# A hand-given instruction order extended through the weight fold and its seam, with TensorE in program order behind it

## The chip, the cores and the metric

One core of one Trainium2 chip. The metric is the device time of one execution in microseconds (us). Every kernel was run several times beside runs of the kernel before on the same chip. Quoted times are medians of the runs; times inside an execution count from the start of its span. A run more than 1.5% above the fastest of its kernel is called slow and is left out of ratios. A ratio is the mean time of one kernel's fast runs over that of the other kernel's fast runs of the same rounds, so it is not quite the ratio of the medians quoted.

In lines of the profile PE is TensorE, PEld its weight loads, DVE VectorE, ACT ScalarE, POOL GpSimd and SP the queue of transfers; L810 is line 810 of that kernel's source. A line of a timeline reads: start and length in us, engine, line, operation, result<-operands, shapes, count; in brackets the engine's idle time just before, and what ended it.

## The reference

```python
def phi(x):                      # polysketch features: products of two sketches, r = 8
    a = einsum('rd,bhsd->bhsr', S1, x); b = einsum('rd,bhsd->bhsr', S2, x)
    return einsum('bhsi,bhsj->bhsij', a, b).reshape(..., r * r)
q_p, k_p = phi(q), phi(k)        # q, k, v: 4 batches, 4 heads, 1088 rows, 32 columns
kv, z = einsum('bhsf,bhsd->bhfd', k_p, v), sum(k_p, axis=2)
x = num(q_p, kv) / (den(q_p, z) + 1e-6)      # then heads side by side: x is 4352 x 128
out = (((x @ w1) * (x @ w2)) @ w3) @ w_out   # d_ff 1024, d_model 128
```

The kernel computes `w3 @ w_out` once (the fold, result `w3o`), so that the end is `((x@w1)*(x@w2)) @ w3o`. It works in groups of 512 rows of x: two halves of each of four batches, then one last group of 256 rows. "x of (1,0)" is the attention output of batch 1, half 0. It is what the third group's products wait for. The way there: on the k side come two small products T and N, which VectorE splits into parts (Ta, Tb; Na, Nb), and kz, the sum over k's features and v; on the q side phi makes the features ph, which TensorE transposes and multiplies by kz to x. A group has 8 "a,b pairs" (`ffn_ab`: two products, a copy on ScalarE, a multiplication on VectorE) and 8 "o products" (`ffn_o`, with `w3o`).

## The kernel before

The w3 weights arrive as raw words. ScalarE makes two tiles of them (`words`), VectorE joins them (`join`, `add`), TensorE transposes (`w3_t`), ScalarE copies, TensorE multiplies by w_out (`w3_mm`):

```python
def words():                                   # in convert(): ScalarE, two passes
    nc.scalar.mul(x["c"], hi.bitcast(F32), 2.0 ** -112)
    nc.scalar.mul(x["m"].bitcast(I32), lo.bitcast(U32), 2.0 ** -29)
...
def w3_t(i):
    ps = psum.tile([128, CW // 128, 128], F32, tag="h", bufs=3, name="ps_wt")
    for c in range(CW // 128):
        nc.tensor.transpose(ps[:, c], w3c[i][:, c * 128:(c + 1) * 128], ident)
    nc.scalar.copy(w3T[ko][:, c0:c0 + CW // 128], ps)
def w3_mm(ko):
    for c in range(NC):
        nc.tensor.matmul(ps, w3T[ko][:, c], wo[:, c], start=(c == 0), stop=(c == NC - 1))
    nc.scalar.copy(w3o[:, ko], ps)
```

A hand-written list of steps (`run_all`) gives the order of the first part. Behind it the source merges streams of steps, and a scheduler may reorder. Dependencies of order, without any semaphore, chain each engine's instructions of the first part, and those behind may only not pass them.

```python
traced = nc.cur_bb.bb.instructions
first_part = len(traced)
run(merge(ffn_steps(1, 16), k_steps(1), w_out))        # the fold; 16 o products are held back
run(merge(ffn_steps(None, 4), q_main(1, 0)))           # the seam: o products beside x of (1,0)
run(merge(ffn_steps(2, 6), q_main(1, 1), rest_steps(1) + k_steps(2)))   # the third group
... # five more groups, last output
for n, ins in enumerate(traced):
    if ins.engine in ordered:
        if ins.engine in last:
            tc.add_manual_dep(ins, last[ins.engine].name, behind, reason="order")
        if n < first_part:
            last[ins.engine] = ins
```

## Time and profile before

| | before |
|---|---|
| time, median of the runs beside the change | 302.19 us |
| span of the profiled run; mean granted TensorE clock | 299.0 us; 0.994 |
| first w3 transpose; last pass of the last `w3_mm` | 59.3; 106.5 us |
| last pass of x of (1,0); of (1,1) | 118.1; 151.5 us |

A line of a table of stretches reads: stretch, its length, then the busy time of TensorE, its weight loads, VectorE, ScalarE and GpSimd, each with its number of instructions, then the granted TensorE clock, the share of DMA and its GB/s.

### The profile page before, as it was taken

The numbers are of one execution on the slowest core, as the hardware profiler recorded it, in microseconds if no ns is written. First come the engines' busy times: TensorE is split into PE (matmuls) and PEld (weight loads), VectorE is DVE, ScalarE is ACT, GpSimd is POOL, SyncE is SP. The second block draws the span as 40 slices with busy tenths as digits, with TensorE's granted clock in tenths as the row PEclk, the third lists the DMA queues.
The fourth block names the chain that finished last, engine by engine and source line by source line (L and its number), as shares of the span: only waits on it lengthen the run. The fifth ranks groups of instructions, "written<-read, shape, count | busy, mean of one in ns | idle before, by whom it ended". The sixth has DMA issues, their size and how long they took to land.

```text
span 299.0 us, 5582 instructions
## 1 busy us (share of the span) xinstructions
PE 282.7 (95%) x2214; PEld 159.8 (53%) x2214; DVE 207.6 (69%) x523; ACT 117.1 (39%) x226; POOL 7.5 (3%) x12
## 2 busy tenths in 40 slices
PE   7987799589999999999999999999999999999994
PEld 5876343267767774545644435464444444444572
DVE  6989779999998985699579329864862583453131
ACT  4634665667886322320242322122423323223122
POOL 0000000000000010010010001000100000000000
PEclk9999999979999999999999999999999999999999
DMA  5649996456744002200100200020002002002020
GB/s 164 211 99 311 254 309 252 134 160 201 246 123 134 0 2 35 71 2 10 30 0 0 35 2 1 2 37 0 2 0 35 2 0 35 1 2 35 0 35 18
DMA packets 28729, 22.37 MB, mean 75 GB/s; under 512 B 20000, under 2 KB 25248, under 8 KB 28704
## 3 DMA queue, kind: packets, MB, share of 16 engines
q1 hardware_dynamic: 28704, 22.03, 26.8%
q8 instruction: 17, 0.28, 0.4%
q14 instruction: 8, 0.07, 0.1%
HBM read 19.80 MB, written 2.23 MB: 74 GB/s over the span
## 4 chain that ended last, share of the span: by engine, by line
PE 80%; DVE 11%; ACT 3%; DMA 2%; issue 1%; SPq 1%; DVEq 0%
PE ps_o L875 19%; PE a_ps L862 19%; PE b_ps L866 18%; PE ps_kvz L557 5%; PE ps_w3o L428 5%; PE ps_x L818 3%; PE ps_wt L421 2%; PE ps_c L725 2%; PE ps_ph L807 2%; DMA k_sb<-in_k_dram 1%; DMA raw<-in_moe_w_dram 1%; PE ps_ab L504 1%; DVE g_k L301 1%; DVE w3c L285 1%; PE ps_c L738 1%
## 5 line engine op out<-in xcount | busy, mean ns | idle before, releaser
L868 DVE TENSOR_TENSOR ab<-ffa,b_ps 128x512 f32<-128x512 f32 (+1 forms) x72 | 47.1, 655 | 64.7 <-PE b_ps L866 62.9
L864 ACT COPY ffa<-a_ps 128x512 f32<-128x512 f32 (+1 forms) x72 | 40.4, 562 | 98.1 <-PE a_ps L862 98.0
L862 PE MATMUL a_ps<-xT,w 128*128 128x512 f32 (+1 forms) x144 | 71.9, 581 | 1.0 <-ACT xT L822 0.7
L866 PE MATMUL b_ps<-xT,w 128*128 128x512 f32 (+1 forms) x144 | 70.3, 570 | 0.0
L875 PE MATMUL ps_o<-ab,w3o 128*128 128x512 f32 (+1 forms) x144 | 70.0, 582 | 0.1
L866 PEld LDWEIGHTS b_ps<-xT,w 128*128 128x128 f32 x144 | 27.2, 190 | 30.1 <-issue 24.9
L875 PEld LDWEIGHTS ps_o<-ab,w3o 128*128 128x128 f32 x144 | 25.3, 189 | 23.9 <-issue 21.6
L862 PEld LDWEIGHTS a_ps<-xT,w 128*128 128x128 f32 x144 | 24.9, 190 | 23.5 <-issue 14.3
L809 ACT COPY pT<-ps_ph 128x512 f32<-128x512 f32 (+1 forms) x18 | 9.2, 565 | 21.0 <-PE ps_ph L807 21.0
L428 PEld LDWEIGHTS ps_w3o<-wo,w3T 128*128 128x128 f32 x128 | 16.5, 205 | 1.5 <-issue 1.2
L428 PE MATMUL ps_w3o<-wo,w3T 128*128 128x128 f32 x128 | 17.0, 289 | 0.0
L269 ACT ACTIVATE cv_c<-raw 128x512 f32<-128x512 f32 x22 | 14.9, 679 | 2.9 <-DVE w3c L282 1.5
L270 ACT ACTIVATE cv_m<-raw 128x512 int32<-128x512 uint32 x22 | 15.0, 681 | 1.8 <-DVE w3c L285 1.5
L421 PE MATMUL ps_wt<-ident,w3c 128*128 128x128 f32 x64 | 10.2, 288 | 4.7 <-DVE w3c L285 4.7
L215 PE MATMUL idle_ps<-zeros 128*128 128x256 bf16 x88 | 12.7, 309 | 1.7 <-DVE zeros L210 1.7
L822 ACT COPY xT<-ps_x 128x512 f32<-128x512 f32 (+1 forms) x9 | 5.1, 563 | 19.0 <-PE ps_x L818 19.0
L421 PEld LDWEIGHTS ps_wt<-ident,w3c 128*128 128x128 f32 x64 | 7.5, 147 | 8.7 <-ACT cv_c L269 4.2
L215 PEld LDWEIGHTS <-zeros 128*128 128x128 bf16 x88 | 9.6, 112 | 3.8 <-DVE zeros L210 1.7
L701 POOL TENSOR_TENSOR q<-qT,q 128x512 f32<-128x512 f32 x5 | 5.9, 1183 | 208.6 <-ACT q L697 208.6
L423 ACT COPY w3T<-ps_wt 128x512 f32<-128x512 f32 x16 | 9.2, 585 | 4.9 <-PE ps_wt L421 4.6
L807 PEld LDWEIGHTS ps_ph<-ident,ph 128*128 128x128 f32 x68 | 7.9, 142 | 5.8 <-issue 4.0
L285 DVE CUSTOM_DVE_ANT_0 w3c<-w3c,cv_m 128x1024 uint16<-128x1024 uint16 x16 | 10.8, 682 | 0.0
(182 smaller groups left out, 343.9 us busy)
## 6 DMA issues: line engine op xcount, KB each, us to landing
raw<-in_moe_w_dram SPq DMA_DIRECT2D x20, 512.0 KB, 5.0
qh<-in_q_dram SPq DMA_DIRECT2D x4, 544.0 KB, 5.8
k_sb<-in_k_dram SPq DMA_DIRECT2D x4, 512.0 KB, 5.2
out_dram<-oT SPq DMA_DIRECT2D x32, 64.0 KB, 1.9
kh<-in_k_dram SPq DMA_DIRECT2D x12, 128.0 KB, 6.4
v_sb<-in_v_dram SPq DMA_DIRECT2D x12, 128.0 KB, 5.1
raw<-in_moe_w_out_dram SPq DMA_DIRECT2D x2, 512.0 KB, 7.7
v_sb<-in_v_dram SPq DMA_DIRECT2D x1, 512.0 KB, 4.9
```

Source lines behind the costliest of these rows:

```text
L215: nc.tensor.matmul(idle_ps[:, :n], zeros[:, :128], zeros[:, :n], start=True, stop=True)
L269: nc.scalar.mul(x["c"], hi.bitcast(F32), 2.0 ** -112)
L270: nc.scalar.mul(x["m"].bitcast(I32), lo.bitcast(U32), 2.0 ** -29)
L421: nc.tensor.transpose(ps[:, c], w3c[i][:, c * 128:(c + 1) * 128], ident)
L428: nc.tensor.matmul(ps, w3T[ko][:, c], wo[:, c], start=(c == 0), stop=(c == NC - 1))
L557: nc.tensor.matmul(out[h * D:(h + 1) * D], lhs, rhs, start=start, stop=stop, skip_group_check=True)
L807: nc.tensor.transpose(ps[:, j * 128:(j + 1) * 128], s["ph"][:, j, 2 * p:2 * p + 2].rearrange("p h i j -> p (h i j)"), ident)
L862: nc.tensor.matmul(a_ps[:, :n], w1[:, cols], xT[key], start=True, stop=True)
L864: nc.scalar.copy(a_sb[:, :n], a_ps[:, :n])
L866: nc.tensor.matmul(b_ps[:, :n], w2[:, cols], xT[key], start=True, stop=True)
L868: nc.vector.tensor_mul(ab[:, :n], a_sb[:, :n], b_ps[:, :n])
L875: nc.tensor.matmul(o_ps[g][:, :n], w3o[:, c], ab_sb.pop((g, c))[:, :n], start=c == 0, stop=c == NC - 1)
```

## The change

Its intent: close TensorE's two gaps at the start of the fold (3.2 and 1.2 us, with a drop of the clock), and order the rest so that no switch between kinds of products is wasted. The hand-written list now goes on through the fold and the seam up to x of (1,0). Behind it TensorE alone keeps program order, and each group's last products come together.

```diff
-        st = []
-        for k in range(len(tiles) + 2):
-            for part, lag in ((0, 0), (1, 1), (2, 2)):
...
+        rounds = []
+        for k in range(len(tiles) + 3):
+            st = [tiles[k][0]] if k < len(tiles) else []      # words
+            if 0 < k <= len(tiles):
+                st += tiles[k - 1][1:3]                        # join, add
+            if k > 2:
+                st += tiles[k - 3][3]                          # w3_t, w3_mm
+            rounds.append(st)
...
+    run_all([g[0], *R[3], g[1], *R[4], *R[5], g[2], *R[6], *R[7], o0[0], *R[8], g[3], *R[9], o0[1], ...
+             *R[17], o0[5], k_kp0, *R[18], o0[6], k_gs0, k_kp1, *R[19], k_kv0, k_gs1, *R[20], k_kv1, k_rg, k_rv, o0[7],
+             k_fin1, g[6], k_next, k_Tm, o1[0], k_Tp, q_tr, q_grid, o1[1], k_Nm, q_lead, g[7], k_Np, q_rem, k_kz, o1[2], ay1, ay2,
+             split, o1[3], o1[4], dens, o1[5], dens2, o1[6], o1[7], phi, phT, nd])
     first_part = len(traced)
-    run(merge(ffn_steps(1, 16), k_steps(1), w_out))
-    run(merge(ffn_steps(None, 4), q_main(1, 0)))
-    run(merge(ffn_steps(2, 6), q_main(1, 1), rest_steps(1) + k_steps(2)))
...
+    def group(g, left, *others):
+        st = ffn_steps(g, left)
+        n = max(len(st) - 4, 0)
+        run(merge(st[:n], *others))
+        run(st[n:])
+    group(2, 6, q_main(1, 1), rest_steps(1) + k_steps(2))
...
-            if n < first_part:
+            if n < first_part or ins.engine == nc.tensor.engine:
```

In the list `g[c]` is the c-th a,b pair of the second group, `o0` and `o1` are the o products of the first and second group, `R[k]` is a round of the fold, `k_` steps are those of batch 1's k, and the rest are those of x of (1,0).

More of the change, by code (lines that the diff above doesn't have):

```diff
@@ L442, in w_out_steps @@
                 continue
-            words, join, add = convert(n, dst, signs=False)
-            tiles.append(([(0.6, words)], [(0.4, join), (0.3, add)], after))
-        st = []
-        for k in range(len(tiles) + 2):
-            for part, lag in ((0, 0), (1, 1), (2, 2)):
-                if 0 <= k - lag < len(tiles):
-                    st += tiles[k - lag][part]
-        return st
+            tiles.append(convert(n, dst, signs=False) + [[f for _, f in after]])
+        rounds = []
[6 more added lines that the diff above has]
+            rounds.append(st)
+        return rounds
     kz_done = {}
@@ L932, in run @@
             f()
-    w_in, w_out = w_in_steps(), w_out_steps()
+    w_in, rounds = w_in_steps(), w_out_steps()
     fs = lambda steps: [f for _, f in steps]
@@ L943 @@
     pause = lambda n: lambda: idle(n)
-    out_st, w_out = fs(w_out[:7]), w_out[7:]
+    out_st = sum(rounds[:3], [])
     run_all([sk_words, sketch_pairs, nat0, nat1, peak, sketch_T, tr0, tr1, ab0, ab1, r_nat, r_tr, first, second,
@@ L950 @@
              out_st[0], n_dens2, f[4], out_st[1], n_phi, f[5], *out_st[2:4], f[6], n_phT, n_nd, *out_st[4:7], f[7]])
+    (k_peak, k_first, k_second, k_tr0, k_tr1, k_ab, k_kp0, k_gs0, k_kv0, k_kp1, k_gs1, k_kv1, k_rg, k_rv,
+     k_fin1, k_next, k_Tm, k_Tp, k_Nm, k_Np, k_kz) = fs(k_steps(1))
+    q_tr, q_grid, q_lead, q_rem, ay1, ay2, split, dens, dens2, phi, phT, nd = fs(q_main(1, 0))
+    g = fs(ffn_steps(1, 16))
+    o0, o1 = ([lambda g=g, c=c: ffn_o(g, c) for c in range(NC)] for g in range(2))
+    pend.clear()
+    R = rounds
+    run_all([g[0], *R[3], g[1], *R[4], *R[5], g[2], *R[6], *R[7], o0[0], *R[8], g[3], *R[9], o0[1], *R[10], *R[11], o0[2],
+             g[4], *R[12], k_peak, o0[3], *R[13], k_first, *R[14], k_second, g[5], *R[15], o0[4], k_tr0, *R[16], k_tr1, k_ab,
+             *R[17], o0[5], k_kp0, *R[18], o0[6], k_gs0, k_kp1, *R[19], k_kv0, k_gs1, *R[20], k_kv1, k_rg, k_rv, o0[7],
+             k_fin1, g[6], k_next, k_Tm, o1[0], k_Tp, q_tr, q_grid, o1[1], k_Nm, q_lead, g[7], k_Np, q_rem, k_kz, o1[2], ay1, ay2,
+             split, o1[3], o1[4], dens, o1[5], dens2, o1[6], o1[7], phi, phT, nd])
     traced = nc.cur_bb.bb.instructions
     first_part = len(traced)
-    run(merge(ffn_steps(1, 16), k_steps(1), w_out))
-    run(merge(ffn_steps(None, 4), q_main(1, 0)))
-    run(merge(ffn_steps(2, 6), q_main(1, 1), rest_steps(1) + k_steps(2)))
-    run(merge(ffn_steps(3, 6), q_main(2, 0)))
-    run(merge(ffn_steps(4, 6), q_main(2, 1), k_steps(3)))
-    run(merge(ffn_steps(5, 6), q_main(3, 0)))
-    run(merge(ffn_steps(6, 6), q_main(3, 1)))
-    run(merge(ffn_steps(7, 6), q_rest()))
+    def group(g, left, *others):
[4 more added lines that the diff above has]
+    group(2, 6, q_main(1, 1), rest_steps(1) + k_steps(2))
+    group(3, 6, q_main(2, 0))
+    group(4, 6, q_main(2, 1), k_steps(3))
+    group(5, 6, q_main(3, 0))
+    group(6, 6, q_main(3, 1))
+    group(7, 6, q_rest())
     run(ffn_steps(8, 2))
```

## The prediction

> **What bounds the kernel now.** I read first the busy shares in 40 slices, to see which engine is full where; then a table of three stretches of my own choosing; then TensorE's and VectorE's instructions in order of time inside them. The page:
>
> ```profile
> PE   7987799589999999999999999999999999999994
> DVE  6989779999998985699579329864862583453131
> PEclk9999999979999999999999999999999999999999
> L868 DVE TENSOR_TENSOR ab<-ffa,b_ps 128x512 f32<-128x512 f32 (+1 forms) x72 | 47.1, 655 | 64.7 <-PE b_ps L866 62.9
> ```
>
> A slice is 7.5 us. TensorE is full from the ninth slice on, and VectorE nearly full from the seventh to the fourteenth (45 to 105 us), the fold of w3 and w_out. VectorE's idle time is nearly all waiting for TensorE, and lies later. The stretches: the fold, its seam to the third group's products, and the third group (columns: length, then busy time of each engine and its instructions).
>
> ```profile
> 54.20:106.60 52.40, 47.75 (x485) 35.43 (x484) 49.41 (x114) 35.36 (x64) 0.00 (x0) 0.97 0.48 142
> 106.60:119.70 13.10, 13.01 (x99) 7.11 (x97) 8.63 (x25) 3.54 (x7) 1.16 (x1) 1.00 0.12 21
> 119.70:153.00 33.30, 33.30 (x362) 17.03 (x361) 25.86 (x67) 8.45 (x16) 1.16 (x1) 1.00 0.11 26
> ```
>
> In the fold both engines are above 90%. In the third group TensorE never stops, and VectorE is at 78%. Why TensorE stops in the fold, from its timeline:
>
> ```profile
> 55.03 1.02 PE L866 MATMUL b_ps<-xT,w 128*128 128x512 f32 x2
> 59.26 0.63 PE L421 MATMUL ps_wt<-ident,w3c 128*128 128x128 f32 x4 [3.20 <-DVE w3c L285]
> 61.09 1.12 PE L421 MATMUL ps_wt<-ident,w3c 128*128 128x128 f32 x4 [1.20 <-DVE w3c L285]
> 62.00 3.09 PE L428 MATMUL ps_w3o<-wo,w3T 128*128 128x128 f32 x16
> ```
>
> It waits 3.2 and 1.2 us for converted w3 tiles, because VectorE did the next batch's k work between them. The 16 passes of L428 that follow take 2.9 us from start to start of the next kind and 1.8 us elsewhere: the clock had dropped (0.66 in the stretch 60 to 65 us). The third group's VectorE work, at its end:
>
> ```profile
> 138.20 1.22 DVE L798 TENSOR_TENSOR ph<-ay,bs 128x1024 f32<-128x1024 f32 x1
> 146.01 0.17 DVE L301 TENSOR_REDUCE g_pair<-ps_T 128x1 f32<-128x8 f32 x1 [1.48 <-PE ps_T L338]
> 149.26 0.17 DVE L301 TENSOR_REDUCE g_pair<-ps_N 128x1 f32<-128x8 f32 x1 [1.05 <-PE ps_N L338]
> 152.28 0.45 DVE L719 STREAM_TRANSPOSE ay_A<-ps_a 128x256 f32<-128x256 f32 x1 [1.46 <-PE ps_a L725]
> ```
>
> Here is a chain phi, T, N, x of some 12 us in which TensorE waits for VectorE and back; TensorE nevertheless shows no gap, since products of the feed-forward part lie between.
>
> **What the Trainium skill says.** "TensorE: Matmul & The Clock Gate", Part 2, step 1: matmuls stay in program order, only weight loads are pulled ahead; its table of specifications calls ScalarE and VectorE strict FIFO. So a given order costs every wait in it; the trace agrees in that no engine passes a waiting instruction. The same page, Part 1, says that an idle window of about 3.4 us halves TensorE's clock; the trace agrees, with the 3.2 us gap and the slow passes after it. "Perfetto Trace Analysis", Optimization Strategy, advises interleaving regimes that have different contended engines. The kernel before does that in the third group; the change takes part of it away.
>
> **The change part by part.** Costs are start-to-start times of the timeline.
>
> (1) No instruction of arithmetic is added or removed; the built orders have 1257 matmul rows each. Two passes of 128x512 take 0.86 us, so an a,b pair (two matmuls) 1.72 and an o product 0.86. Leaving and re-entering these for 32-row or 32-column products costs 0.09 + 0.10 us (passes of 0.523 and 0.533 in place of 0.43). Such excursions behind the third group's x number 18 before and 19 after by the built orders: nothing there.
>
> (2) The fold, from the second group's first product (54.2) to its successor's x at 118.6. TensorE's work in the order given now: 8 a,b pairs 13.7, 16 o products 13.7, 64 transposes of w3 7.0, 128 passes of L428 14.3, k products 5.7, q products with ph and x 4.0, excursions 1.6: 60.0 us. Before has done 12 of those 16 o products by 118.6, so 56.6 us of work in 64.4: there are 7.8 us to win, and no more.
> VectorE's work in the same stretch: 16 tiles at 1.79 (0.45 + 0.73 + 0.61, they depend on each other) 28.6, 8 ab 4.9, k 12.9, q 8.8, two output transposes 1.3: 56.5 us. Two engines with 60.0 and 56.5 us cannot both run in fixed order without waits.
> I walked the given order by hand, with landing 0.2 us after the last pass and 0.6 us for a ScalarE copy. Gone are the 3.2 and 1.2 us gaps: the first w3 transpose can start at 58.6. But a new loop comes: a pair of w3 tiles needs ScalarE to do copy, next tile's two words (1.14), copy, and only then the second half of L428 runs; each words step itself waits for the VectorE step two rounds back, since its tiles have two buffers. The walk gives 4.7 to 6.6 us a pair, 5.8 on average, so 40.5 us from the first to the last of the eight L428 sums, against 41.6 in the trace (64.9 to 106.6). The last sum ends at 105.8 instead of 106.6, with four more o products done and two a,b pairs and T, N fewer: about the same work. The gain of the fold proper is then near nothing.
> At the seam the given order has waits that before doesn't: T behind fin1, which stands behind the output transpose (1.2 us); ay1 and ay2 behind Np, which stands behind the eighth ab (1.0 + 0.8); phi behind the second output transpose, which stands behind the last of five o products (2.2); then ph, copy, x, copy with no product left to fill (1.5). Some 6.5 us. Walk: phi done at 126.6, x at 129.5. I take 127 for x, as such a walk adds up its own small errors. Before, with the 4 o products done too, would be at 118.6 + 3.4 = 122.0. So +5.0 us.
>
> (3) The third group. All 16 o products are now used up in the given part, and VectorE's later work may not start before its last instruction, phi. From there it has, in its built order up to phi of the next half: q and k transposes and maxima 5.7, then 2.7 + 5.5 + 5.7 + 3.4: 23 us. Then gA, gB, T, its pair, N, its pair, x (in T's and N's single PSUM buffer): 11 us as in the trace, where phi's end at 139.4 to x's end at 152.0 is 12.6. With 1.4 us of waiting for the first products that is 35.4 from phi; the first x ends 2.9 behind its phi, so from one x to the next about 32.5 us, as long as before (118.6 to 152.0). But in it TensorE has only 6 a,b pairs (10.3 us), where before had 8 pairs and 8 o products (20.6). TensorE idles some 12 us, in a gap before ph near 6 us and gaps around N near 5. At x's end: 127 + 32.5 = 159.5 against 152.0, and 2 pairs and 4 o products (6.9 us) still to do that before has behind it. The sum: 7.5 + 6.9 = 14.4 us.
>
> (4) Behind it TensorE is the bound again and its order hardly matters; in the fifth group x stands right behind N with Np between, 1.5 us. The clock may drop at the 6 us gap, which the fold's no longer does: taken as even. I take off 2 us for what VectorE's order may save, since I counted nothing in its favour. Sum +14 us.
>
> **The rivals.** (a) The fold runs as its author meant it: no gaps, all of the 7.8 us. Then x comes at 114.2 instead of 127, and the third group still gives back: 14 - 12.8 = about +1, so the same within 2%. For it: the clock drop and both long gaps vanish. Against: ScalarE's copies behind words, three PSUM buffers for four kinds of products, VectorE at 56.5. (b) The third group's idle does not come, because VectorE's order there is shorter than I count. The trace before shows its 29 us from first ab (121.7) to N's pair (150.8), with only 3 us of waits; TensorE order cannot shorten that. If still 5 us were saved: 311. (c) Program order behind saves switches and waits of x: at most 0.5 us. (d) My walk is right to the letter, and the clock drops: 127 becomes 129.5, +17 to +19: 321.
>
> **The range and the chances.** 302.3 + 14 = 316 us. Rival (b) with half of (a)'s gain gives 308 and (d) with one more clock drop 323: that is the range. 2% slower begins at 308.4. Only the whole of (a) keeps it within 2%, and faster needs (a) and (b) together. Chances: faster 0.02, same 0.08, slower 0.90.
>
> **What would show it.** Step 2: no TensorE gap over 1 us between 54 and 61, clock 1.00 there; gaps of 0.4 to 1.3 us inside L428's 16 passes, released by ScalarE's w3T copy; the last L428 at 104 to 107; x of the second half-batch ending at 124 to 130. Step 3: TensorE busy under 75% in the 32 us behind that x, gaps released by ph on VectorE and by Ts, while VectorE is above 85% there; no o product in it. Step 4: TensorE above 99% from the fourth group on. I am wrong if that x lands before 118, or if TensorE has less than 6 us of idle time in the third group.

## More of the kernel before

The experiments ran in rounds on several chips, and the kernel before has medians of 301.4 to 302.9 us in them; differences in us between kernels of different rounds therefore carry about 1 us, and the ratios, each to its own before, are the safer measure.

The fold once more, in the bounds that all later kernels are shown in:

```profile
54.20:107.00 52.80, 48.15 (x490) 35.82 (x488) 49.55 (x115) 35.59 (x66) 0.00 (x0) 0.97 0.47 141
```

The chain that ended last is TensorE's for four fifths, VectorE's for a ninth:

```profile
PE 80%; DVE 11%; ACT 3%; DMA 2%; issue 1%; SPq 1%; DVEq 0%
```

## The result, and the profile after

| | before | after |
|---|---|---|
| median | 302.19 us | 331.48 us |
| runs | 300.95 to 303.18 | 328.04, 328.45; slow: 334.51, 334.63 |
| ratio of fast runs (95% interval) | | 1.0864 (1.0794 to 1.0934) |
| span profiled; clock | 299.0; 0.994 | 326.7; 0.974 |
| last pass of the last `w3_mm` | 106.5 us | 107.4 us |
| last pass of x of (1,0) | 118.1 | 132.1 |
| last pass of x of (1,1) | 151.5 | 166.4 |

The change makes the kernel slower, by nearly twice what was predicted. The 27.7 us between the spans split along TensorE's own order: the first product behind x of (1,0) starts 14.7 us later (118.6 to 133.3; x itself ends at 118.7 and 132.7); from there to the first product behind x of (1,1) it takes 1.4 more (34.8 against 33.4); and 11.6 are added behind that. Again the shares in slices come first, here 40 of 8.2 us.

```profile
PE   7987899698889968895679999998999999999994
DVE  7899788957986468899512943985394393373231
PEclk9999999999999999998658999999999999999999
```

Before, TensorE was full from the ninth slice on; now it has holes from the eighth slice to the twenty-first, and the clock is low in slices 19 to 22, down to about half in the third of them. The stretches, from the fold to the end:

```profile
54.20:107.00 52.80, 45.39 (x403) 30.74 (x402) 39.88 (x66) 31.91 (x60) 0.00 (x0) 1.00 0.32 101
134.00:168.00 34.00, 25.50 (x338) 13.96 (x338) 26.18 (x75) 7.86 (x14) 2.54 (x2) 0.84 0.06 18
168.00:326.00 158.00, 152.66 (x876) 74.90 (x876) 80.05 (x185) 42.18 (x78) 4.47 (x4) 0.98 0.06 12
```

In the fold, VectorE did 39.88 us of work where before it did 49.55, with 66 instructions in place of 115, in the same time and with the fold itself ending only 0.9 us later. Of those 9.7 us, 1.3 are two multiplications of a,b pairs; nearly all the rest is k and q work on the way to x of (1,0) and of the halves behind it, which now comes later. In the third group (134 to 168 us) TensorE is busy for three quarters of the time. Where it waits (TensorE's timeline; in brackets the idle time just before and what ended it):

```profile
120.54 0.33 PE L660 MATMUL ps_kz<-ident,kvm 128*128 128x128 f32 x1 [3.13 <-DVE Nb L323]
129.48 1.39 PE L810 MATMUL ps_ph<-ident,ph 128*128 128x128 f32 x8 [1.47 <-DVE ph L801]
153.80 1.94 PE L810 MATMUL ps_ph<-ident,ph 128*128 128x128 f32 x8 [3.75 <-DVE ph L801]
163.02 0.39 PE L336 MATMUL ps_N<-Ta,P 128*128 128x8 f32 x2 [2.63 <-DVE Tb L323]
165.46 1.97 PE L821 MATMUL ps_x<-pT,kz 128*64 128x512 f32 x4 [1.52 <-DVE Nb L323]
```

Every one is released by VectorE: the chain phi, ph, T, N, x of the prediction. In the chain that ended last VectorE's share rose from 11 to 20%:

```profile
PE 70%; DVE 20%; ACT 6%; issue 3%; DVEq 0%; ACTq 0%
```

Inside the fold the loop that the prediction walked is there. ScalarE's timeline (first fence) and TensorE's (second) of the same 5 us:

```profile
72.86 0.59 ACT L424 COPY w3T<-ps_wt 128x512 f32<-128x512 f32 x1
74.00 0.69 ACT L269 ACTIVATE cv_c<-raw 128x512 f32<-128x512 f32 x1 [0.55 <-ACT w3T L424]
74.74 0.67 ACT L270 ACTIVATE cv_m<-raw 128x512 int32<-128x512 uint32 x1
75.31 0.57 ACT L424 COPY w3T<-ps_wt 128x512 f32<-128x512 f32 x1
```

```profile
73.19 0.60 PE L422 MATMUL ps_wt<-ident,w3c 128*128 128x128 f32 x4
73.63 1.06 PE L429 MATMUL ps_w3o<-wo,w3T 128*128 128x128 f32 x8
75.93 1.16 PE L429 MATMUL ps_w3o<-wo,w3T 128*128 128x128 f32 x8 [1.25 <-ACT w3T L424]
```

The transposes of the second half are done soon after 73.6, but ScalarE, in its given order, must first make both words of the next tile. The copy starts at 75.31 and TensorE goes on at 75.93, after 1.25 us. Over the fold, from the first transpose to the last `w3_mm`, TensorE's gaps of every kind add up to 6.3 us.

### The profile page after: what moved, and what is told of

The parts are those of the page before. It is cut to its first block, busy times and chain, and to the rows that moved or that the text cites. A ratio compares the mean times of both kernels' runs of the same rounds, so it can differ in the third digit from the quotient of the medians.

```text
span 326.7 us, 5588 instructions
## 1 busy us (share of the span) xinstructions
PE 291.6 (89%) x2214; PEld 161.8 (50%) x2214; DVE 211.3 (65%) x523; ACT 116.4 (36%) x226; POOL 7.7 (2%) x12
## 4 chain that ended last, share of the span: by engine, by line
PE 70%; DVE 20%; ACT 6%; issue 3%; DVEq 0%; ACTq 0%
PE ps_o L878 18%; PE a_ps L865 17%; PE b_ps L869 16%; PE ps_kvz L560 4%; PE ps_x L821 3%; DVE ab L871 2%; PE ps_w3o L429 2%; PE ps_ph L810 2%; PE ps_c L728 2%; DVE w3c L282 2%; PE idle_ps L215 2%; DVE ph L801 1%; DVE w3c L281 1%; ACT cv_c L269 1%; ACT cv_m L270 1%
## 5 line engine op out<-in xcount | busy, mean ns | idle before, releaser
L865 PE MATMUL a_ps<-xT,w 128*128 128x512 f32 (+1 forms) x144 | 74.0, 596 | 1.0 <-ACT xT L825 0.7
L878 PE MATMUL ps_o<-ab,w3o 128*128 128x512 f32 (+1 forms) x144 | 71.3, 590 | 0.7 <-ACT w3o L430 0.7
L869 PE MATMUL b_ps<-xT,w 128*128 128x512 f32 (+1 forms) x144 | 71.9, 581 | 0.0
L869 PEld LDWEIGHTS b_ps<-xT,w 128*128 128x128 f32 x144 | 27.9, 194 | 32.2 <-issue 27.5
L865 PEld LDWEIGHTS a_ps<-xT,w 128*128 128x128 f32 x144 | 25.8, 196 | 25.3 <-issue 16.9
L429 PE MATMUL ps_w3o<-wo,w3T 128*128 128x128 f32 x128 | 17.8, 283 | 4.5 <-ACT w3T L424 4.2
L429 PEld LDWEIGHTS ps_w3o<-wo,w3T 128*128 128x128 f32 x128 | 15.5, 191 | 6.3 <-ACT w3T L424 5.9
L810 PE MATMUL ps_ph<-ident,ph 128*128 128x128 f32 x68 | 10.3, 293 | 6.9 <-DVE ph L801 6.7
L821 PE MATMUL ps_x<-pT,kz 128*64 128x512 f32 (+1 forms) x48 | 11.7, 526 | 3.9 <-DVE Nb L323 3.1
L882 DVE STREAM_TRANSPOSE oT<-ps_o 128x512 f32<-128x512 f32 x8 | 5.7, 717 | 14.4 <-PE ps_o L878 14.4
## 6 DMA issues: line engine op xcount, KB each, us to landing
kh<-in_k_dram SPq DMA_DIRECT2D x12, 128.0 KB, 4.3
v_sb<-in_v_dram SPq DMA_DIRECT2D x12, 128.0 KB, 5.2
```

Of the source, the lines that this page charges most:

```text
L810: nc.tensor.transpose(ps[:, j * 128:(j + 1) * 128], s["ph"][:, j, 2 * p:2 * p + 2].rearrange("p h i j -> p (h i j)"), ident)
L821: nc.tensor.matmul(view(ps[64 * p:64 * (p + 1)]), kz_done[t if b is None else b][:, 64 * p:64 * (p + 1)], view(s["pT"][:, p, :n]), start=T ...
L865: nc.tensor.matmul(a_ps[:, :n], w1[:, cols], xT[key], start=True, stop=True)
L869: nc.tensor.matmul(b_ps[:, :n], w2[:, cols], xT[key], start=True, stop=True)
L878: nc.tensor.matmul(o_ps[g][:, :n], w3o[:, c], ab_sb.pop((g, c))[:, :n], start=c == 0, stop=c == NC - 1)
```

## The experiments

In the expectations, theory L is the prediction's own account (x of (1,0) late through the waits at the seam, then an idle third group with its o products used up; the fold proper costing about 1 us). F says that the given order of the fold itself is the main loss, R that it is TensorE's program order behind, and D and O, named later, split F. All 18 runs of experiments computed the right result.

### Which part: the given list or the program order behind

**TensorE free behind the given list** (the change without its last line):

```diff
-            if n < first_part or ins.engine == nc.tensor.engine:
+            if n < first_part:
```

> The changed kernel with one thing undone: behind the hand-given part TensorE is again ordered by the scheduler. Theory L (the loss is made in the hand-given part: its waits lengthen VectorE's chain by some 15 us, and it uses up the o products that would fill the third group): the scheduler can move only two a,b pairs and a few o products of the third group into its gaps, so some 7 us of left-over work and the slow clock go, 317 to 323 us. Rival R (program order behind is what costs): nearly all of the 29 us comes back, 302 to 306 us.

314.82 us, ratio to before 1.0455 (1.0411 to 1.0498), below what L expected and far above what R did. So about half the loss is the program order behind, the other half the list.

**Program order alone**, on the kernel before: the opposite edit.

> The kernel before with that one thing added: TensorE in program order behind its own, shorter hand-given part. Theory L: o products still lie in the third group, so only small waits around N and x come, 302 to 309 us. Rival R: 318 to 331 us.

309.08 us, ratio 1.0264 (1.0219 to 1.031), at the upper edge of L and far from R. By itself it costs 7.6 us, and in company some 13 (328.2 for the fast runs, less 314.8, is 13.4; by the ratios it is 12.3). The reason is in the trace: TensorE, forbidden to pass a waiting instruction, has new gaps of 2.01, 1.62 and 1.62 us and another 3.4 us at half clock. The first gap:

```profile
117.55 2.39 PE L875 MATMUL ps_o<-ab,w3o 128*128 128x512 f32 x4 [2.01 <-DVE oT L879]
```

An o product that waits for the output buffer which VectorE's transpose empties holds up everything behind it.

**The seam rearranged**, TensorE still in order behind. N's split (`k_Np`) moves ahead of the last a,b pair and that pair ahead of ScalarE's q step (`q_lead`), kz goes behind ay2, and phi ahead of the last two o products:

```diff
-   ... k_Tp, q_tr, q_grid, o1[1], k_Nm, q_lead, g[7], k_Np, q_rem, k_kz, o1[2], ay1, ay2,
-   split, o1[3], o1[4], dens, o1[5], dens2, o1[6], o1[7], phi, phT, nd])
+   ... q_tr, o1[1], k_Nm, q_grid, k_Np, g[7], q_lead, q_rem, o1[2], ay1, ay2, k_kz,
+   split, o1[3], o1[4], dens, o1[5], dens2, phi, o1[6], o1[7], phT, nd])
```

> The changed kernel with the tail of the hand-given order rearranged: Np before the eighth ab, the ffa copy before ScalarE's q steps, kz behind ay2, phi before the last two o products. Theory L: the 3.1 us gap before kz and most of the 1.5 us gap before ph vanish, and since VectorE's chain sets the end all of it is kept: 3 to 5 us faster than the changed kernel. If the slow clock is what sets the end, or program order: within 1 us.

326.84 us, ratio 1.0829 (1.0788 to 1.0871). x of (1,0) came 4.1 us sooner (128.0), but only a part of it reached the end: x of (1,1) was 2.6 us sooner (163.75) and the end of the profiled run 2.0, with half-clock periods of 20.5 us in it.

**Each round's products and their copy ahead of its words**, against the 1.25 us waits:

```diff
+            st = list(tiles[k - 3][3]) if k > 2 else []
+            if k < len(tiles):
+                st.append(tiles[k][0])
...
-            if k > 2:
-                st += tiles[k - 3][3]
```

> The changed kernel with each round's w3 products (and so ScalarE's copies of them) put ahead of that round's words on ScalarE. Theory L: the waits of the L429 passes for the w3T copy (4.5 us in TensorE's matmul row) shrink and the fold ends 2 to 5 us earlier, 2 to 5 us faster in all. Rival: ScalarE then waits for TensorE and VectorE gets its words later; same or slower by up to 3 us.

330.81 us, ratio 1.0982 (1.0929 to 1.1036). The waits shrank and the fold ended 1.2 to 1.7 us sooner, but the gaps at the seam then fell together and the clock was at half from 118.6 us for 10 us. All four runs lie at clocks of 0.951 to 0.958, so this was not a fair test of the copies.

### The clock, and the o products used up early

**No products held back together** (`n = len(st)` in `group`).

> The changed kernel with each group's products merged to the last as before, none held back behind the other work (the part 'each step's products together' undone alone). Theory L: the third group gets one more a,b pair ahead of ph, and o products around N and x in place of nothing; 320 to 326 us. If holding back is harmless: 327 to 332.

330.43 us: 323.24 at a clock of 0.978, three slow runs of 330.2 to 331.4 at 0.952 to 0.962. Each cluster lies 4 to 5 us below the like one of the change (328 and 334.5), but with one fast run there is no interval. It stays open.

**Idle products in the third group's gaps**: 60 products of zeros in bfloat16, 128x256, nobody reads them; they only keep TensorE busy.

> The changed kernel with 60 bf16 matmuls on zeros of 128x256[...] put into the third group's gaps, 30 ahead of ph, 20 ahead of N, 10 ahead of x: useless work where TensorE stands idle. Theory C (a good part of the loss is the half clock that the gaps bring on, and it is also in VectorE's chain, since the T, c5, N steps run at half speed): the clock stays at 1.0 behind 150 us, 5 to 9 us faster than the changed kernel's fast runs, 319 to 323. Against C (half clock only where TensorE waits anyway): within 2 us of 328.

328.08 us: 322.34 at a clock of 1.000, 326.84 at 0.981, and two at 329.3 and 0.971. No interval either, but the four runs line up with their clocks.

**Idle products in all the larger gaps behind 115 us**, with the same edit extended to the seam and the fifth group:

> The changed kernel with useless bf16 matmuls in all its larger gaps behind 115 us (ahead of kz, ph, kt, ph, N, x, and of the fifth group's x), so that the clock has no reason to drop. Theory C: granted clock at 0.995 or more in every run, and 320 to 323 us, 6 to 12 below the changed kernel's own runs, with no second cluster at 334. Against C: 327 or more.

325.61 us (324.42 to 327.34), clock 0.989 to 0.998, ratio 1.0824 (1.0774 to 1.0875). The slow cluster at 334.5 is gone. So the lowered clock costs the slow runs of the change about 9 us. For the fast ones the difference is 2.6 us, or 1.2 by the ratios, whose intervals overlap: it is not shown. The idle products are work of their own on TensorE, so neither figure is exact.

**The last four o products of the second group left to the third**:

```diff
-             split, o1[3], o1[4], dens, o1[5], dens2, o1[6], o1[7], phi, phT, nd])
+             split, o1[3], dens, dens2, phi, phT, nd])
+    pend += [(1, c) for c in range(4, NC)]
```

> The changed kernel with the last four o products of the second group taken out of the hand-given order and left to the third group, as the kernel before has them. Theory L: phi no longer waits for the second output transpose (1.4 us), the third group's gap ahead of ph is filled and the clock stays up: 319 to 325 us. If the lost products are of no account (VectorE's chain and in-order waits set all): 326 to 332 us.

330.09 us, ratio 1.093 (1.0885 to 1.0975), clocks 0.956 to 0.966: nothing gained, but with 27 us at half clock in the profiled run. Whether the o products or the clock hid the gain, the next run tells.

**Both: four held back, and idle products in the gaps.**

> The same with the last four o products of the second group held back for the third group. If used-up o products cost time of their own: 3 to 5 us below the run with the clock kept alone, 315 to 318. If VectorE's chain sets all: equal within 1.5 us.

322.55 us, ratio 1.0718 (1.0679 to 1.0757), clocks 0.989 to 1.0. With the clock kept up, holding back four o products gains 3.1 us (325.61 less 322.55). The idle products are not the same in the two kernels, though: 55 in place of 24 ahead of the first ph, 25 and 15 in place of 30 and 20 in the third group, in another PSUM buffer, so a part of the 3.1 us may be theirs. The prediction's account of the third group is right in kind. But 21 us of the loss are still there: theory L cannot be the whole.

### The given list taken apart

**The list ends with the fold**: the same order up to `o0[7]`, everything behind it as in the kernel before, with the second group's eight o products left over.

> The hand-given order ends with the fold (behind the first group's last o product); from there all is the scheduler's as before, with the eight o products of the second group left to it. Theory L (the fold proper costs about 1 us; the seam, the used-up o products and program order make the rest): 301 to 306 us. Rival F (the given order of the fold costs too, since VectorE has not run ahead with the third group's k work): 308 to 313 us.

314.32 us, ratio 1.0445 (1.0413 to 1.0477). Here theory L fell. Neither the seam's list nor used-up o products of the second group nor program order behind are left in this kernel, and it loses as much as the one with all of the list (314.8). F had expected even less loss, up to 313.

```profile
54.20:107.00 52.80, 45.54 (x403) 30.84 (x402) 40.29 (x66) 32.37 (x61) 0.00 (x0) 1.00 0.32 100
```

The fold looks as in the change, down to VectorE's 66 instructions. Its last `w3_mm` is at 107.5, a mere 1 us later than before; but x of (1,0) comes at 135.9. The fold pays later: just before that x TensorE stands still for 5.91 us until VectorE has made ph, and the clock was at half from 128.8 us for 6.8.

```profile
132.51 2.06 PE L810 MATMUL ps_ph<-ident,ph 128*128 128x128 f32 x8 [5.91 <-DVE ph L801]
```

**The rearranged seam, TensorE free behind**:

> Both undone: the rearranged tail of the hand-given order, and TensorE free behind it. If the two losses add (seam some 4 us, program order behind some 13): 309 to 312 us. If freedom behind already makes up for the seam: 314 to 316, as with freedom alone.

311.2 us, ratio 1.0322 (1.0273 to 1.0371): the seam's arrangement is worth 3.6 us (4.0 by the ratios) with TensorE free behind, as expected if the two losses add.

Now which engine's order in the list? Theory D: VectorE and ScalarE, fixed, cannot run ahead with later work. Rival O: TensorE's own order and its o products used up. In each of the next kernels some engines are exempt from the list, from the fold's start to its end; TensorE is free behind. The edit, here for VectorE:

```diff
+    first_old = len(nc.cur_bb.bb.instructions)        # ahead of the fold
...
-            if n < first_part or ins.engine == nc.tensor.engine:
+            if n < first_old or n < first_part and ins.engine != nc.vector.engine:
```

**TensorE alone keeps the list:**

> Compared with e1 (given order on every engine through the seam, TensorE free behind it, 314.8 us): here TensorE alone keeps the given order through the fold and the seam; VectorE, ScalarE, GpSimd and SyncE take what is ready. Theory D (the fixed order keeps VectorE and ScalarE from running ahead with the third group's k and q work in the fold): 301 to 308 us, VectorE's busy time in the fold 47 us or more against 39.9, x of (1,1) at most at 158 us. Rival O (TensorE's own given order, with the o products used up by x of (1,0)): 312 to 316 us, VectorE's busy time in the fold may rise but x of (1,1) stays at 162 or later.

302.8 us beside 302.49 of before, ratio 1.0028 (0.9938 to 1.0118). TensorE's given order, used-up o products included, costs nothing that these runs can show (their interval reaches to 3.6 us). This is what theory D expected.

```profile
54.20:107.00 52.80, 49.33 (x482) 33.75 (x480) 49.02 (x99) 34.51 (x65) 0.00 (x0) 1.00 0.47 139
```

TensorE's order is that of the change, yet it does 4 us more work in the stretch, since VectorE and ScalarE deliver sooner; and VectorE has run ahead again (49.02 us).

**TensorE alone free:**

> TensorE free throughout, the other engines keep the given order through the fold and the seam. Theory D: 311 to 316 us, VectorE still at about 40 us of work in the fold. Rival O: 301 to 308 us, with o products left over behind x of (1,0) as in the kernel before.

310.15 us, ratio 1.0222 (1.0143 to 1.0301). A little under D's range: TensorE, free to take other products while it waits, hides 4.7 of the 13 us (7 by the ratios). It does not contradict the run before; it shows that either side of a wait may give way.

**VectorE alone free:**

> All engines given through the seam but VectorE, which takes what is ready; TensorE free behind the seam. If it is VectorE's order alone (theory D in its narrow form): 301 to 308 us, VectorE's busy time in the fold 47 us or more. If ScalarE's order holds VectorE back as well (its k and q steps come through ScalarE): 308 to 313. Rival O: 312 to 316 us.

308.19, 309.03 and 311.14 us; a fourth run took 722 and is told under the skill's last section. Ratio 1.022 (1.0128 to 1.0312): VectorE's order is not the whole, the second of the expectations. A further run at the same kernel, for a usable profile:

> The same kernel as the run with VectorE alone free. The other executions of it took 308 to 311 us: here 308 to 311 too, with VectorE's busy time in the fold between the 42 us of the kernel with the given order and the 49 us of the one with TensorE alone given. If the 720 us come back, they belong to this kernel and not to that execution.

308.86 us; VectorE's work in the fold is up to 44.28 us, between the two as expected:

```profile
54.20:107.00 52.80, 47.34 (x472) 32.72 (x471) 44.28 (x85) 31.96 (x62) 0.00 (x0) 1.00 0.30 101
```

**ScalarE alone free:**

> ScalarE alone free, all others given through the seam, TensorE free behind. VectorE's order still holds back the third group's k work, so at most half is won: 308 to 314 us. Under 307 would say that ScalarE's order is the whole cause; 314 or more that ScalarE's order counts only once VectorE is free.

307.63 us, ratio 1.0186 (1.0138 to 1.0234), just under the expected range: ScalarE's order weighs about as much as VectorE's (the intervals of the two ratios overlap).

```profile
54.20:107.00 52.80, 47.75 (x475) 32.98 (x474) 40.27 (x67) 33.37 (x62) 0.00 (x0) 1.00 0.30 101
```

Here VectorE has not run ahead (40.27 us), and still 7 us are won. So VectorE's missing work is not the only carrier: the w3T copy no longer stands behind two words, the last `w3_mm` comes at 103.8 in place of 107.4, TensorE's gaps in the fold fall to 4.1 us. The same spot of TensorE's timeline:

```profile
71.44 1.06 PE L429 MATMUL ps_w3o<-wo,w3T 128*128 128x128 f32 x8
73.02 1.16 PE L429 MATMUL ps_w3o<-wo,w3T 128*128 128x128 f32 x8 [0.53 <-ACT w3T L424]
```

**VectorE and ScalarE free**, TensorE, GpSimd and SyncE given (does the order of the loads matter?):

> VectorE and ScalarE free in fold and seam; TensorE, GpSimd and SyncE (loads and stores) keep the given order; TensorE free behind. If ScalarE's order holds the second half: 301 to 305 us. If the order of the loads and stores holds it: 307 to 311 us, as with VectorE free alone.

303.5 us, ratio 1.0043 (1.0003 to 1.0082). VectorE has run ahead again:

```profile
54.20:107.00 52.80, 49.98 (x483) 34.12 (x481) 48.36 (x96) 35.76 (x67) 0.00 (x0) 1.00 0.30 101
```

Against the kernel with TensorE alone given (1.0028) nothing is left that these runs can show for the loads' order; the two engines make up the whole. From the list's 314.8 the gains are 5.8 us for VectorE (309.0, the median of the fast runs), 7.2 for ScalarE, and 11.3 for both together. By the ratios they are 7.1, 8.1 and 12.4: together less than the sum.

How this reaches the end is seen with the first w3 transpose as zero, which takes out the different starts (columns: to the last pass of x of (1,0); from there to x of (1,1); from there to the end; us, one profiled run each):

| kernel | x of (1,0) | x of (1,1) | end | sum |
|---|---|---|---|---|
| before | 58.8 | 33.4 | 147.5 | 239.7 |
| whole list, TensorE free behind | 77.0 | 33.5 | 143.7 | 254.2 |
| VectorE free | 70.2 | 32.8 | 145.4 | 248.4 |
| ScalarE free | 68.5 | 33.8 | 143.7 | 246.0 |
| both free | 65.2 | 30.8 | 147.3 | 243.2 |
| TensorE alone given | 64.9 | 28.3 | 148.1 | 241.2 |
| the change | 73.4 | 34.3 | 160.2 | 267.9 |

The loss appears at x of (1,0) and, with VectorE's and ScalarE's order free, is taken back partly there and partly in the third group. TensorE has about 4.3 us more of its work done by x of (1,0) (five o products of 0.86 us) in the six lower rows than in before, which for this column compares as 63.1. The clock is in this column too: up to x of (1,0) it was at half for 6.8 us with the whole list, for 3.4 in before and in the rows with VectorE or both free, and not at all in the others. Of the whole list's 77.0 us up to 3.4 may be that. The last row shows the program order: with it, the waits of the third group cannot be filled with other products, and the end is 16.5 us further from x of (1,1) than with TensorE free behind.

### A shorter list

What the change set out to do is done by its beginning alone. The list is extended over four rounds only, with the copy ahead of the words; the rest is left to the scheduler, as is TensorE behind:

```diff
+    run_all([g[0], *R[3], g[1], *R[4], *R[5], g[2], *R[6]])
...
     first_part = len(traced)
+    run(merge(st1[3:], k1, w_rest))
+    run(merge(ffn_steps(None, 4), q_main(1, 0)))
+    run(merge(ffn_steps(2, 6), q_main(1, 1), rest_steps(1) + k_steps(2)))
...
+            if n < first_part:
```

> A version meant to beat both: the hand-given order goes on only over the second group's first three products and the first pair of w3 tiles, where the kernel before has its gaps of 3.2 and 1.2 us and its slow clock; from there the scheduler, with all o products left to it. If those gaps are true losses on TensorE: 2 to 6 us faster than before, 296 to 300 us. If VectorE's work in the fold sets the end and the gaps are only where it shows: 300 to 306 us.

299.03 us (298.9 to 300.87) beside 302.48, ratio 0.9907 (0.9861 to 0.9953): the one kernel that beats before, by about 1%, clear of noise. How much of it is the short list and how much the copies ahead of the words was not tested.

```profile
54.20:107.00 52.80, 51.27 (x492) 35.24 (x491) 48.67 (x108) 35.38 (x66) 0.00 (x0) 1.00 0.48 141
```

TensorE 51.27 us busy of 52.8 at full clock, and VectorE nearly as far ahead as before.

## Why the prediction was right or wrong

The direction was right, the size about half of what came: 316 us with a range to 323 was predicted, and the fast runs took 328. Its steps against the profiled run (span difference 27.7 us, predicted 13.9):

1. **No change of arithmetic.** The page counts 2214 TensorE products before and after. Right.
2. **The fold and the seam, x at 127.** The step that failed. The walk saw what was there: the first gap gone (0.84 us in place of 3.2), full clock, waits of 0.46 to 1.25 us in the passes of w3 by w_out released by ScalarE's copy, waits at the seam. The last sum came at 107.4 and not at 105.8; x ended at 132.7, and the product behind it started at 133.3. Of the 6.3 us from 127 to 133.3, 1.6 are the fold, 2.2 the seam (mainly the 3.13 us gap before kz, where 1.8 had been counted, and 0.7 of waiting for the copy of x), and 2.5 were in the walk's own 129.5 and shaded away for no reason that a view supported. (A small misreading beside it: by 118.6 us before had done 11 of the 16 o products and not 12; the twelfth starts at 118.62.) More important than the sum is the cause. The prediction laid the late x to 6.5 us of waits in the seam's given order, and "The gain of the fold proper is then near nothing" was read as a cost near nothing too. It compared TensorE's work done by the same time. It did not compare VectorE's, 9.7 us less. With the list ended before the seam x still comes at 135.9, and the kernel is 12.9 us slower than before (314.3 against 301.4). With the longer list, through the seam, the loss goes away once VectorE and ScalarE are free (302.8 with only TensorE's order kept).
3. **The third group.** In kind right: no o product and six a,b pairs in it, TensorE at 75%, gaps released by ph, Tb and Nb on VectorE, 6.9 us of work left over (two pairs, four o products). TensorE's idle time was 9.0 us where some 12 were predicted. From x to x it took 34.8 where 32.5 was predicted; a part of the 2.3 is the half clock, which the prediction took as even. But the used-up o products alone do not empty the third group: with the same list and TensorE free behind, the scheduler puts eight a,b pairs and eight o products between the two x, and no gap over 0.7 us is left. "VectorE above 85%" was wrong: 26.18 of 34 us, 77%, as it waits for TensorE in turn.
4. **Behind.** "Its order hardly matters" failed. The wait of x for N in the fifth group came as predicted (1.62 us), but taking the program order away gains some 13 us: from x of (1,0) to the last output's 0.7 us, that kernel's trace has but two gaps, 0.68 and 0.23 us, where the change has 10.2 us of them between 150 us and the fifth group's x. The prediction had these gaps in its sum, as idle time, without seeing that they come from program order. The clock, "taken as even", cost an estimated 2.7 us behind x of (1,1), where it was at half for 5.8 us. And "I take off 2 us" was a hedge with nothing behind it.

The sum of the misses: 6.3 + 2.3 + 2.7 + 2.0 and 0.5 in small terms (0.1 of it in the fifth group's wait) are the 13.8 us.

Of the rivals, (a) did not come: the fold kept 6.3 us of gaps. (b) did not come. (c) had the wrong sign. (d), the walk to the letter with a drop of the clock, was the nearest, at 321; with idle products for the clock the change ran in 322.3 in one run and 324.4 to 327.3 in four.

What is shown: the two halves of the loss (list, program order behind), that the list's half lies in VectorE's and ScalarE's order, and some 9 us of clock in the slow runs. Not cleanly separated: the clock's share in the fast runs (1 to 3 us), and the 3.1 us for four used-up o products, as the idle products differed too. What is argued only: that the 49 instructions missing from VectorE's fold are by themselves what makes VectorE's free order worth some 6 us. With ScalarE free the same 48 are missing and the kernel still gains 7, so the count of VectorE's work is a sign of the lost freedom, not a measure of the time. Open: the part of the products held together, and whether ScalarE's share is the copy behind two words alone; the run for that, the copies moved ahead with TensorE free behind, was not made.

## What to carry to other kernels

In this kernel a fixed order for TensorE cost nothing measurable up to x of (1,0) as long as the engines that feed it could take what was ready. A fixed order for those engines took away their freedom to run ahead, and this was paid one or two stages later. So judge a stage not only by when it ends, but also by how much of the next stage's work every engine has done by then. In a case like this, give the order by hand only over the few waits it is meant to close, here four rounds, and leave the rest free.

## What the Trainium skill lacked or had wrong

- "TensorE: Matmul & The Clock Gate", Part 1 (What's actually happening), has the activity window as free-running, 3413 ns. The traces agree: all half-clock periods that end within a run last about 3.4, 6.8, 10.2, 13.7 or 17.1 us. The page has the ramp at the start vary from run to run; what it lacks is what this does to comparisons, since like gaps may or may not cost a period. After the 3.13 us gap at 117.4 us the change kept full clock; after the 3.14 us gap at 118.4 the kernel with held-back o products (without idle ones) ran 13.7 us at half. The change itself ran in two clusters, 328 us at 0.974 and 334.5 at 0.952. The page's table has the clock fall after at least one idle window of about 3.4 us. A gap of a whole window was not needed here: the change's second half-clock period, 10.2 us from 163.6, began just behind a single gap of 2.63 us, and the one in the kernel before, at 61.0, with gaps of 3.20 and 1.20 us. The prediction took that 3.2 us gap as agreement; it is a little shorter than the window.
- The same page, Seeing it yourself, warns that clock events are unreliable and that the gate has been seen stuck for over 50 us. One execution here fits that and goes further, though a stuck gate is not shown: the kernel with VectorE free once took 722 us, with no clock event recorded at all (so that the summary gives 1.000), while TensorE's products took 2.5 times their usual busy time (180.6 us for the b products against 71.9 in the change) and VectorE's were unchanged. The same kernel took 308 to 311 us in its other four runs. Below are the group of the b products and the line of the clock of that execution, and then the same group in the change.

```profile
L869 PE MATMUL b_ps<-xT,w 128*128 128x512 f32 (+1 forms) x144 | 180.6, 1364 | 0.0
```

```profile
core 0: 720.4 us, clock 1.000
```

```profile
L869 PE MATMUL b_ps<-xT,w 128*128 128x512 f32 (+1 forms) x144 | 71.9, 581 | 0.0
```

- "Perfetto Trace Analysis", Optimization Strategy, says to find the gaps of the engine that one optimizes and what blocks it. It lacks the counterpart: work that a feeding engine did not do ahead need not leave a gap of its size in the stage where it is missing. With the list ended at the fold, TensorE's idle time in the fold's stretch (54.2 to 107) was 7.3 us against 4.7 before; the kernel's loss was 12.9 us.
- No page says what it costs to fix the order of an engine. Here, on top of TensorE's own, which cost nothing measurable: ScalarE's and VectorE's orders from 54 to 133 us cost 11.3 us together.
